# Attention, a max network and a gated network in one kernel: one operand block and two sums of the second pair are made during the product for y, and raw blocks, h's parts and g's stores are issued at other steps

## The chip, the cores and the metric

The kernel runs on one core of a Trainium2 chip. A core has five engines with a queue of instructions each: TensorE (PE: matmuls, with its weight loads PEld beside them), VectorE (DVE), ScalarE (ACT), GpSimd (POOL) and SyncE (SP), which here does nothing but issue DMAs. Each queue is worked off in order, and an instruction that waits holds all that stand behind it. The metric is the device time of one execution in microseconds (us): 1137.37 us, the median of 3 runs (1137.26 to 1139.59).

## The reference, cut to what matters

```python
def _attn_ref(q, k, v, cap):                    # 4 batches, 12 heads, 448 rows, head 64
    scores = cap * np.tanh(np.matmul(q, k.transpose(0, 1, 3, 2)) / np.sqrt(64) / cap)
    attn = np.exp(scores - np.max(scores, axis=-1, keepdims=True))
    return np.matmul(attn / (np.sum(attn, axis=-1, keepdims=True) + 1e-09), v)

x = attn_out.transpose(0, 2, 1, 3).reshape(1792, 768)
h = np.maximum(np.maximum(x @ w1, x @ w2), x @ w3)      # 768 x 768 each (float64 weights)
y = h @ w_out                                            # 1792 x 768
g = y @ w_gate                                           # 768 x 1536
out = (g * (1 / (1 + np.exp(-g))) * (y @ w_val)) @ moe2_w_out   # 1792 x 768
```

## The kernel before, in words

Each product is made of three fp32r matmuls: an operand is cut into a high part (ACT copies it to fp32r) and a low part (DVE or POOL subtracts the high part), and high x high, high x low and low x high are added up in PSUM. `parts_of` (L493 to L498) is the helper that cuts, so ACT's halves of all cuts have line L495 and those of DVE and POOL L498.

The weights are stored as float64. A raw block of 768 KB is fetched by SP (`fetch`, L455), and turned into fp32 in four steps, `one` to `four` (L469 to L486): ACT takes the absolute value of the high words (L470), DVE clamps and shifts (L475, L476), DVE puts the sign in and scales the low words (L479, L482), POOL adds both (L485). There are two buffers for raw blocks. So the fetch of block u+1 waits on SP until POOL's add of block u-1 has read its buffer.

The stages, in the order of time:

- 0 to 105 us: attention for batch 0, one pair of heads after the other, each in four slots. Per pair SP issues the loads of k, q and v (L82, L85, L74), the sums of the exponentials (`su`, L302), their inverses (`rd`, L313) and the inverses spread over the partitions (`rb`, L318). POOL multiplies by `rb` and cuts x (`finish`, L328 to L331). One conversion step of a raw block stands at the end of each slot.
- 105 to 420 us: attention for batch b+1, woven with x @ w1, w2, w3 of batch b. Block conversions and POOL's cuts of weights run beside it.
- 420 to 527 us: x @ w1, w2, w3 of batch 3. h was stored in DRAM by batch; it is fetched again (`hr`) and cut into `ha` (`split_h`, L646).
- 528 to 623 us: y = h @ w_out for batches 0 to 3, six products of 18 matmuls each. Batches 0 and 1 form pair 0, batches 2 and 3 pair 1.
- 623 to 948 us: the products for g and the value, in Strassen's form (Winograd's variant, 7 products in place of 8): per pair of batches seven operands B11, T2, T3, T1, B21, T4, B22 in `yo`, made of y's blocks `yf` by four sums (`sums_of_y`, L702), each cut in three slices; and per column block c = 0 to 11 seven weight operands (`ops_steps`). A product has 9 matmuls (`product`, L817). For c = 0 all seven products of pair 0 come first, then those of pair 1; from c = 1 on the pairs alternate.
- 948 to 1136 us: the last product, out = g @ w_out, of g read back from DRAM (`gr`) and cut.

The order of the work is written out by hand (tile pools set the waits for buffers). In the y stage, the cuts of h of batch b+1 stand one behind each product of batch b (L764 to L767). Pair 0's operands are made behind the last three products of batch 1 (L773 to L779): per slice a cut of B22, four sums and the cuts of T2, T3, T1 and T4, on POOL, ACT and DVE. Pair 1's are made by `y_steps` (L797 to L804) after the last product for y, behind the products of pair 0. Their buffer `yo1` lies where the pools of the y stage were.

Of the kernel before, what the change touches and what calls it, by code (L numbers as in the profile page):

```python
# [25 lines left out]
def attention_max_silu_kernel(ctx, tc, q, k, v, cap, w1, w2, w3, w_out, wg, wv, wo, out):  # L26
# [18 lines left out]
    nc = tc.nc  # L45
# [8 lines left out]
    capt = const.tile([P, 1], F32, name="capt")  # L54
    acap = const.tile([P, 1], F32, name="acap")
    ncap = const.tile([P, 1], F32, name="ncap")
    qsc = const.tile([P, 1], F32, name="qsc")
# [55 lines left out]
def program(ctx, tc, tensors, shared, general):  # L113
# [482 lines left out]
    with tc.manual_schedule():  # L596
# [49 lines left out]
        def split_h(b, kk):  # L646
# [4 lines left out]
            if kk + 4 < NF1:  # L651
                fetch_h(b, kk + 4)
# [49 lines left out]
        def sums_of_y(p, kk):  # L702

            b11, b12, b21, b22 = yf[p, 0, kk], yf[p, 1, kk], yf[p, 0, kk + 3], yf[p, 1, kk + 3]
            return dict(T1=b11, T3=b12, T2=b22, T4=b21), [
                lambda eng: less(eng, b11, b12, b11), lambda eng: less(eng, b12, b22, b12),
                lambda eng: less(eng, b22, b22, b11), lambda eng: less(eng, b21, b21, b22),
# [36 lines left out]

        events = {(0, 0): [split_next, convert_part], (0, 1): [convert_part]}
# [9 lines left out]
        for b in range(B):  # L755
            p, x = divmod(b, 2)
            for i in range(NK):
# [13 lines left out]
                if b == 0:  # L771
                    yo_part(0, "B11" if e < 3 else "B21", kk, y)
                if b == 1 and e >= 3:  # L773
# [4 lines left out]
                    for name, eng in zip(("T2", "T3", "T1", "T4"), (ve, po, ve, po)):  # L778
                        yo_part(0, name, kk, at[name], eng)  # L779
# [222 lines left out]
```

## Time and profile before

| what | value |
|---|---|
| median of 3 runs | 1137.37 us |
| the profiled execution: its time, its span | 1138.13 us, 1136.2 us |
| PE busy | 1090.2 us, 96% of the span |
| PE's weight loads busy | 941.3 us, 83% |
| DVE, POOL busy | 682.3 us, 682.7 us: 60% each |
| ACT busy | 510.1 us, 45% |

The execution is 1.9 us longer than the span, which runs from the first to the last instruction. A PE that is busy 96% of the time leaves 46 us in which it stood still; where these lie is read from the stretches of time below. A busy PE can still be slow: the granted clock (PEclk, 1.00 is 2.4 GHz) tells that.

### The profile page before, as it was taken

The page shows a single profiled execution, that of the slowest core. Times are in us where ns is not written, and L with a number is a line of the kernel's source. Part 1 is how long each engine was busy: PE and PEld are TensorE (multiplying, and loading weights), DVE is VectorE, ACT ScalarE, POOL GpSimd, SP SyncE. Part 2 cuts the span into 40 slices and gives each one's busy share as a digit, 9 for nine tenths or more (in the row PEclk, how much of TensorE's full clock was granted, in tenths as well). Part 3 has the DMA queues.
Part 4 walks back from the last instruction along what each step waited for, and adds up shares of the span by engine and source line. Part 5 has one row for each costly group of instructions (what it writes and reads, how often), then busy time and mean ns, then how long its engine had stood idle before and what let it go on. Part 6 is the DMA issues. An engine that isn't in the chain of part 4 may idle for free.

```text
span 1136.2 us, 15037 instructions
## 1 busy us (share of the span) xinstructions
PE 1090.2 (96%) x5480; PEld 941.3 (83%) x5480; DVE 682.3 (60%) x865; ACT 510.1 (45%) x789; POOL 682.7 (60%) x577
## 2 busy tenths in 40 slices
PE   7998998999999999999989789999999998999998
PEld 5444777888888889998979679999999998999997
DVE  2574999977776678764373956666676755211210
ACT  4876666677666762453353433323323224211210
POOL 1367999899878789985263566666655555211210
PEclk8999999999999999999989989999999999999999
DMA  4565444433434323443122022222232226333232
GB/s 113 134 170 134 118 122 125 131 101 105 135 106 118 116 82 117 161 129 105 33 78 66 0 89 88 88 99 103 92 112 98 88 82 192 97 110 100 84 93 64
DMA packets 167683, 118.67 MB, mean 104 GB/s; under 512 B 85680, under 2 KB 162992, under 8 KB 167600
## 3 DMA queue, kind: packets, MB, share of 16 engines
q1 hardware_dynamic: 167600, 117.62, 34.5%
q8 instruction: 45, 0.74, 0.3%
q14 instruction: 38, 0.31, 0.1%
HBM read 90.67 MB, written 26.82 MB: 103 GB/s over the span
## 4 chain that ended last, share of the span: by engine, by line
PE 76%; DVE 9%; POOL 4%; DMA 4%; ACT 3%; issue 2%; SPq 1%; DVEq 0%; POOLq 0%; ACTq 0%
PE ps_g L826 25%; PE ps_h L544 20%; PE ps_o L896 14%; PE ps_y L544 7%; PE pv L281 6%; PE sc L232 4%; POOL xp L328 1%; DVE el L256 1%; DVE yo L498 1%; DMA rb<-rd 1%; ACT e L246 1%; DMA raw<-in_moe_w_dram 1%; DVE xp L328 1%; DMA wo<-wod 1%; POOL yf L700 1%
## 5 line engine op out<-in xcount | busy, mean ns | idle before, releaser
L544 PE MATMUL ps_h<-x,ws 128*128 128x448 f32 x1296 | 294.3, 374 | 0.0
L544 PEld LDWEIGHTS ps_h<-x,ws 128*128 128x128 f32 x1296 | 241.1, 190 | 38.6 <-issue 18.1
L826 PE MATMUL ps_g<-yo,o_S 128*128 128x448 f32 x864 | 184.2, 369 | 4.5 <-DVE yo L498 1.9
L498 POOL TENSOR_TENSOR ws<-w,ws 128x384 fp32r<-128x384 f32 x144 | 181.7, 1269 | 10.6 <-ACT ws L495 1.6
L896 PE MATMUL ps_o<-wo,g 128*128 128x384 f32 x1008 | 177.3, 336 | 5.1 <-ACT g L495 2.7
L896 PEld LDWEIGHTS ps_o<-wo,g 128*128 128x128 f32 x1008 | 176.0, 189 | 6.5 <-ACT g L495 3.1
L826 PEld LDWEIGHTS ps_g<-yo,o_S 128*128 128x128 f32 x864 | 162.8, 189 | 21.7 <-DVE yo L498 2.6
L485 POOL TENSOR_TENSOR t<-t,raw 128x768 uint32<-128x768 uint32 x42 | 81.8, 1948 | 107.3 <-DVE raw L482 100.6
L826 PE MATMUL ps_g<-yo,o_A 128*128 128x448 f32 x648 | 140.0, 370 | 4.9 <-POOL yo L498 3.4
L826 PEld LDWEIGHTS ps_g<-yo,o_A 128*128 128x128 f32 x648 | 122.1, 189 | 18.2 <-POOL yo L498 4.2
L256 DVE TENSOR_TENSOR el<-e,eh 128x896 fp32r<-128x896 f32 x64 | 86.7, 1357 | 45.0 <-ACT eh L255 39.4
L498 POOL TENSOR_TENSOR g<-gr,g 128x384 fp32r<-128x384 f32 x28 | 32.5, 1181 | 113.0 <-ACT g L495 113.0
L246 ACT ACTIVATE e<-e,ncap,acap 128x896 f32<-128x896 f32 x96 | 99.4, 1036 | 0.6
L544 PE MATMUL ps_y<-ha,ws 128*128 128x448 f32 x432 | 90.8, 373 | 5.6 <-ACT ha L495 3.2
L238 ACT ACTIVATE e<-sc,qsc 128x896 f32<-128x896 f32 x96 | 86.7, 904 | 17.6 <-PE sc L232 17.4
L544 PEld LDWEIGHTS ps_y<-ha,ws 128*128 128x128 f32 x432 | 83.1, 193 | 13.3 <-ACT ha L495 3.5
L497 POOL TENSOR_SCALAR ws<-w 128x384 fp32r<-128x384 f32 x108 | 87.5, 810 | 0.2
L281 PE MATMUL pv<-eh,vs 128*128 128x448 f32 (+1 forms) x256 | 78.6, 389 | 2.5 <-ACT o L297 2.5
L498 DVE TENSOR_TENSOR g<-gr,g 128x384 fp32r<-128x384 f32 x28 | 23.9, 860 | 75.7 <-ACT g L495 75.5
L485 POOL TENSOR_TENSOR w<-w,raw 128x768 uint32<-128x768 uint32 x18 | 37.9, 2108 | 40.8 <-DVE raw L482 40.8
L470 ACT ACTIVATE t<-raw 128x768 f32<-128x768 f32 x42 | 37.6, 895 | 51.6 <-DMA raw<-in_moe_w_val_dram 42.7
L732 POOL TENSOR_TENSOR t<-t,t 128x384 f32<-128x384 f32 x36 | 39.9, 1109 | 31.2 <-DVE o_A L498 31.1
(113 smaller groups left out, 1560.9 us busy)
## 6 DMA issues: line engine op xcount, KB each, us to landing
raw<-in_moe_w_dram SPq DMA_DIRECT2D x18, 768.0 KB, 4.6
raw<-in_moe_w_out_dram SPq DMA_DIRECT2D x18, 768.0 KB, 5.0
gr<-gd SPq DMA_DIRECT2D x14, 768.0 KB, 4.9
raw<-in_moe_w_gate_dram SPq DMA_DIRECT2D x12, 768.0 KB, 4.3
raw<-in_moe_w_val_dram SPq DMA_DIRECT2D x12, 768.0 KB, 4.5
qn<-in_q_dram SPq DMA_DIRECT2D x48, 112.0 KB, 3.5
rb<-rd SPq DMA_DIRECT2D x48, 112.0 KB, 3.1
h<-ht SPq DMA_DIRECT2D x24, 224.0 KB, 2.0
```

Of the source, the lines that this page charges most:

```text
L232: nc.tensor.matmul(ps[:, j, :S], a[r, cols_], m[r], start=i == 0, stop=i == 2)
L238: nc.scalar.activation(ee[n][:, :w], ps[:, :w, :S], AF.Tanh, scale=qsc)
L246: nc.scalar.activation(t, t, AF.Exp, bias=ncap, scale=acap)
L256: nc.vector.tensor_sub(lo, t, f(hi))
L281: nc.tensor.matmul(pv[g][j][:, :S], a, m, start=c == 0 and x == 0, stop=c == 3 and x == len(ops) - 1,)
L485: nc.gpsimd.tensor_tensor(t, t, low, op=ALU.add)
L497: copier.tensor_scalar(hi, src, 1.0, 1.0, ALU.mult, ALU.mult)
L498: subtracter.tensor_tensor(lo, src, f(hi), op=ALU.subtract)
L544: nc.tensor.matmul(ps, a, m, start=kk == 0 and n == 0, stop=kk == NK - 1 and n == 2)
L732: nc.gpsimd.tensor_tensor(a[x], a[x0], a[x1], op=op)
L826: nc.tensor.matmul(ps, a[:, s0, k3], m[:, kk, s1], start=kk == 0 and j == 0, stop=kk == 2 and j == 2,)
L896: nc.tensor.matmul(po[s][x][:, :HW], a, m[:, x * HW : (x + 1) * HW], start=c == 0 and n == 0, stop=c == NF2 - 1 and n == 2,)
```

## The change

It has these parts:

1. B11 of pair 1 gets a buffer of its own (`b11_p`) that is there during the y stage. It is cut behind batch 2's first three products.
2. Pair 1's sums 0 (b12 - b11) and 1 (b12 - b22) are made by DVE behind batch 3's products (`early_sums`). After the y stage there remain: B22, sum 2, T2, T3, T1, B21 with sum 3, T4, all on ACT and DVE. Before, POOL had the subtractions for B22 and T4 and the sums 1 and 3.
3. h's blocks of batch b+1 are cut two at a time behind the first three products of batch b, and the first three are fetched one batch ahead. There are 3 fetch buffers in place of 4.
4. The fetch of the next raw block stands behind step `one` in place of step `clamp`, that is one step earlier.
5. The stores of g wait in a list and are issued up to two products later; around the last column block the fetch of g comes one step earlier and its cut one step later.
6. Four constants share one tile.

```diff
         def one():
             nc.scalar.activation(f(t), high.bitcast(F32), AF.Abs)
-
-        def clamp():
             if count[0] < min(count[1] + 2, len(real)):
                 fetch()
+
+        def clamp():
...
+        b11_p = pool(b11_pools, "b11", 1).tile([P, 3, 2, S], F32R, name="b11")
...
+        def early_sums(e, kk):
+
+            if e < 3:
+                made[kk] = sums_of_y(1, kk)
+                made[kk][1][0](nc.vector)
+            if (1, 1, kk) in yf and (1, 1, kk + 3) in yf:
+                made[kk][1][1](nc.vector)
...
-                if 1 <= b < B - 1:
-                    if i == 0:
-                        fetch_all(b + 1)
-                    split_h(b + 1, i)
+                if 1 <= b < B - 1 and i < 3:
+                    split_h(b + 1, 2 * i)
+                    split_h(b + 1, 2 * i + 1)
+                if b < B - 2 and i == 4:
+                    fetch_all(b + 2)
...
-                if b == 0:
-                    yo_part(0, "B11" if e < 3 else "B21", kk, y)
+                if x == 0 and (p == 0 or e < 3):
+                    yo_part(p, "B11" if e < 3 else "B21", kk, y)
+                if b == B - 1:
+                    early_sums(e, kk)
...
         y_steps = [
-            lambda: (y_part("B11"), y_sum(0, nc.vector)),
-            lambda: (y_part("B22", nc.gpsimd), y_sum(1, nc.gpsimd)),
-            lambda: y_sum(2, nc.vector),
-            lambda: y_part("T2"),
+            lambda: y_part("B22"), lambda: y_sum(2, nc.vector), lambda: y_part("T2"),
             lambda: y_part("T3"), lambda: y_part("T1"),
-            lambda: (y_part("B21"), y_sum(3, nc.gpsimd)), lambda: y_part("T4", nc.gpsimd),
+            lambda: (y_part("B21"), y_sum(3, nc.vector)), lambda: y_part("T4"),
         ]
...
+            while len(stores) > 1:
+                store()
...
-                nc.sync.dma_start(out=gd[:, c, 2 * p * S : (2 * p + 1) * S], in_=t[3])
+                stores.append((gd[:, c, 2 * p * S : (2 * p + 1) * S], t[3]))
...
-                at.setdefault(10, []).append(lambda: (fetch_g(rows[0]), fetch_g(rows[1])))
-                at.setdefault(12, []).append(lambda: [split_g(rows[0], y) for y in range(4)])
+                at.setdefault(8, []).append(lambda: [store() for _ in [*stores]])
+                at.setdefault(9, []).append(lambda: (fetch_g(rows[0]), fetch_g(rows[1])))
+                at.setdefault(13, []).append(lambda: [split_g(rows[0], y) for y in range(4)])
```

On DVE, at the end of batch 1's products for y, the kernel before has this (`yo0` are pair 0's operands, `ha2` the cut h of batch 2, `yf1_3` the y block 3 of batch 1):

```order
L498 TENSOR_TENSOR ha2_5512<-hr2_3_5510,ha2_5512 128x448
L498 TENSOR_TENSOR yo0_5319<-yf1_3_5588,yo0_5319 128x448
L700 TENSOR_TENSOR yf1_3_5588<-yf1_3_5588,yf0_0_5345 128x448
L498 TENSOR_TENSOR yo0_5319<-yf1_3_5588,yo0_5319 128x448
L498 TENSOR_TENSOR yo0_5319<-yf0_0_5345,yo0_5319 128x448
L498 TENSOR_TENSOR ha2_5512<-hr2_4_5515,ha2_5512 128x448
L498 TENSOR_TENSOR yo0_5319<-yf1_4_5625,yo0_5319 128x448
L700 TENSOR_TENSOR yf1_4_5625<-yf1_4_5625,yf0_1_5376 128x448
L498 TENSOR_TENSOR yo0_5319<-yf1_4_5625,yo0_5319 128x448
L498 TENSOR_TENSOR yo0_5319<-yf0_1_5376,yo0_5319 128x448
L498 TENSOR_TENSOR ha2_5512<-hr2_5_5540,ha2_5512 128x448
```

The changed kernel has there:

```order
L496 TENSOR_TENSOR ha2_5511<-hr2_3_5514,ha2_5511 128x448
L496 TENSOR_TENSOR ha2_5511<-hr2_4_5518,ha2_5511 128x448
L496 TENSOR_TENSOR ha2_5511<-hr2_5_5543,ha2_5511 128x448
L496 TENSOR_TENSOR yo0_5320<-yf1_3_5593,yo0_5320 128x448
L702 TENSOR_TENSOR yf1_3_5593<-yf1_3_5593,yf0_0_5346 128x448
L496 TENSOR_TENSOR yo0_5320<-yf1_3_5593,yo0_5320 128x448
L496 TENSOR_TENSOR yo0_5320<-yf0_0_5346,yo0_5320 128x448
```

The last two cuts of batch 2's h moved from behind pair 0's operands to the front of them.

On DVE, at the step from the y stage to the products for g, the kernel before has (`o0_S2` is a weight operand of c = 0, `yo1` are pair 1's operands, `yf2_0` and `yf3_0` y blocks of batches 2 and 3):

```order
L498 TENSOR_TENSOR o0_S2_5919<-t79_5792,o0_S2_5919 128x384
L498 TENSOR_TENSOR yo1_6012<-yf2_0_5710,yo1_6012 128x448
L498 TENSOR_TENSOR yo1_6012<-yf2_1_5737,yo1_6012 128x448
L498 TENSOR_TENSOR yo1_6012<-yf2_2_5764,yo1_6012 128x448
L700 TENSOR_TENSOR yf2_0_5710<-yf3_0_5972,yf2_0_5710 128x448
L700 TENSOR_TENSOR yf2_1_5737<-yf3_1_5999,yf2_1_5737 128x448
L700 TENSOR_TENSOR yf2_2_5764<-yf3_2_5866,yf2_2_5764 128x448
L700 TENSOR_TENSOR yf3_3_5889<-yf3_3_5889,yf2_0_5710 128x448
L700 TENSOR_TENSOR yf3_4_5914<-yf3_4_5914,yf2_1_5737 128x448
L700 TENSOR_TENSOR yf3_5_5943<-yf3_5_5943,yf2_2_5764 128x448
L837 TENSOR_TENSOR qn1_64<-ps_g0_0_1_6048,qn0_63 128x448
```

The changed kernel has there:

```order
L702 TENSOR_TENSOR yf2_1_5746<-yf3_1_6010,yf2_1_5746 128x448
L702 TENSOR_TENSOR yf3_1_6010<-yf3_4_5922,yf3_1_6010 128x448
L496 TENSOR_TENSOR o0_S2_5927<-t79_5803,o0_S2_5927 128x384
L496 TENSOR_TENSOR yo1_6025<-yf3_3_5899,yo1_6025 128x448
L496 TENSOR_TENSOR yo1_6025<-yf3_4_5922,yo1_6025 128x448
L496 TENSOR_TENSOR yo1_6025<-yf3_5_5951,yo1_6025 128x448
L702 TENSOR_TENSOR yf3_3_5899<-yf3_3_5899,yf2_0_5713 128x448
L702 TENSOR_TENSOR yf3_4_5922<-yf3_4_5922,yf2_1_5746 128x448
L702 TENSOR_TENSOR yf3_5_5951<-yf3_5_5951,yf2_2_5775 128x448
L864 TENSOR_TENSOR qn1_61<-ps_g0_0_1_6051,qn0_60 128x448
```

Two sums of the last y block now stand ahead of the weight operand S2; B11's cuts are gone from here and B22's, which POOL made, stand in their place, with three sums in place of six.

On SP, in the attention of batch 0, the kernel before has (`vp0` is v of a pair of heads, `raw3` a raw block of weights):

```order
L85 DMA vp0_179<-in_v_dram 64x64
L302 DMA su2_580<-o2_554 112x1x4 x2
L318 DMA rb1_583<-rd1_186 64x448 x2
L455 DMA raw3_588<-in_moe_w1_dram 128x6x128
L82 DMA kn0_65<-in_k_dram 128x3x64
```

The changed kernel has there:

```order
L83 DMA vp0_176<-in_v_dram 64x64
L453 DMA raw3_567<-in_moe_w1_dram 128x6x128
L300 DMA su2_579<-o2_551 112x1x4 x2
L316 DMA rb1_582<-rd1_183 64x448 x2
L80 DMA kn0_62<-in_k_dram 128x3x64
```

The raw block, which waits for POOL's add of the block before last, moved ahead of the sums and of the spread inverses.

## Rows read from the trace of the kernel before

**Rows 1.** The profile's page: its first line

```profile
span 1136.2 us, 15037 instructions
```

**Rows 2.** Stretches: length; PE, PEld, DVE, ACT, POOL busy (instructions); PEclk, DMA share, GB/s

```profile
0.00:100.00 100.00, 89.07 (x397) 48.53 (x398) 49.01 (x78) 69.83 (x82) 39.30 (x45) 0.95 0.55 139
100.00:210.00 110.00, 100.35 (x492) 79.08 (x493) 97.33 (x98) 71.68 (x92) 103.46 (x84) 0.94 0.44 123
...
575.00:585.00 10.00, 5.15 (x14) 4.36 (x15) 7.67 (x7) 5.00 (x11) 8.48 (x7) 0.70 0.08 23
...
635.00:670.00 35.00, 25.60 (x104) 20.34 (x103) 22.91 (x37) 14.73 (x29) 19.09 (x17) 0.90 0.05 20
...
945.00:980.00 35.00, 29.89 (x156) 28.32 (x155) 12.56 (x13) 13.06 (x22) 18.16 (x12) 0.95 0.59 181
```

**Rows 3.** Timeline, PE, y stage: start, us, instruction, count, [idle before <- releaser]

```profile
527.89 47.10 PE L544 MATMUL ps_y<-ha,ws 128*128 128x448 f32 x231 [0.72 <-DVE ht L570]
...
578.15 0.47 PE L544 MATMUL ps_y<-ha,ws 128*128 128x448 f32 x1 [3.17 <-ACT ha L495]
580.32 2.24 PE L544 MATMUL ps_y<-ha,ws 128*128 128x448 f32 x5 [1.70 <-DVE ha L498]
```

**Rows 4.** Timeline, PE, first products for g

```profile
623.44 2.00 PE L826 MATMUL ps_g<-yo,o_A 128*128 128x448 f32 x9
...
655.48 3.35 PE L826 MATMUL ps_g<-yo,o_A 128*128 128x448 f32 x8 [3.40 <-POOL yo L498]
...
667.38 2.93 PE L826 MATMUL ps_g<-yo,o_S 128*128 128x448 f32 x13 [0.50 <-DVE o_S L498]
```

**Rows 5.** The chain that ended last: start, us, what

```profile
138.69 5.52 DMA raw<-in_moe_w_dram
...
181.76 4.46 DMA raw<-in_moe_w_dram
...
667.38 273.70 PE ps_g L826 x1330
```

**Rows 6.** Timeline, DVE, around the y stage's end

```profile
567.11 0.63 DVE L700 TENSOR_TENSOR yf<-yf,yf 128x448 f32<-128x448 f32 x1
...
624.69 0.56 DVE L498 TENSOR_TENSOR o_S<-t,o_S 128x384 fp32r<-128x384 f32 x1 [2.68 <-ACT o_S L495]
...
628.60 8.10 DVE L700 TENSOR_TENSOR yf<-yf,yf 128x448 f32<-128x448 f32 x6
...
637.16 1.68 DVE L498 TENSOR_TENSOR yo<-yf,yo 128x448 fp32r<-128x448 f32 x3
```

**Rows 7.** Timeline, POOL, the same place

```profile
643.46 1.83 POOL L485 TENSOR_TENSOR t<-t,raw 128x768 uint32<-128x768 uint32 x1 [7.78 <-DVE raw L482]
...
653.21 1.13 POOL L851 TENSOR_TENSOR kn<-kn,qn 128x448 f32<-128x448 f32 x1
654.30 3.31 POOL L498 TENSOR_TENSOR yo<-yf,yo 128x448 fp32r<-128x448 f32 x3
```

**Rows 8.** Timeline, SP and POOL, one pair of heads in batch 0

```profile
50.92 1.85 POOL L485 TENSOR_TENSOR w<-w,raw 128x768 uint32<-128x768 uint32 x1
...
52.02 1.93 SPq L302 DMA_DIRECT2D su<-o  x2
...
54.05 1.19 SPq L318 DMA_DIRECT2D rb<-rd  x2
...
55.33 0.54 SPq L455 DMA_DIRECT2D raw<-in_moe_w_dram  x1
...
56.92 2.95 POOL L328 TENSOR_TENSOR xp<-o,rb 64x448 f32<-64x448 f32 x2 [4.15 <-DMA rb<-rd]
...
61.88 1.86 POOL L485 TENSOR_TENSOR w<-w,raw 128x768 uint32<-128x768 uint32 x1
```

**Rows 9.** Timeline, the step to the last product: PE

```profile
951.16 5.57 PE L896 MATMUL ps_o<-wo,g 128*128 128x384 f32 x22 [2.73 <-ACT g L495]
957.54 17.26 PE L896 MATMUL ps_o<-wo,g 128*128 128x384 f32 x98 [0.82 <-DVE g L498]
```

More of the change, by code (lines that the diff above doesn't have):

```diff
@@ L53, in attention_max_silu_kernel @@
     ident = const.tile([P, P], F32, name="ident")
[L54 to L57, printed above, removed]
+    four = const.tile([P, 4], F32, name="four")
+    capt, acap, ncap, qsc = (four[:, i : i + 1] for i in range(4))
     qn = [const.tile([P, 4, 2, D], F32, name=f"qn{i}") for i in range(2)]
@@ L657, in fetch_all @@
         def fetch_all(b):
-            for kk in range(4):
+            for kk in range(3):
                 fetch_h(b, kk)
@@ L702, in sums_of_y, with b2 @@
         def sums_of_y(p, kk):
[L704 to L707, printed above, removed]
+            b11, b12 = yf[p, 0, kk], yf[p, 1, kk]
+            def b2(x):
+                return yf[p, x, kk + 3]
+            return dict(T1=b11, T3=b12, T2=lambda: b2(1), T4=lambda: b2(0)), [
+                lambda eng: less(eng, b11, b12, b11), lambda eng: less(eng, b12, b2(1), b12),
+                lambda eng: less(eng, b2(1), b2(1), b11), lambda eng: less(eng, b2(0), b2(0), b2(1)),
             ]
@@ L743, in ops_steps @@
             ]
+        def early_sums(e, kk):
[4 more added lines that the diff above has]
+                made[kk][1][1](nc.vector)
+        made = {}
         events = {(0, 0): [split_next, convert_part], (0, 1): [convert_part]}
@@ L783, in program @@
         yo1_pools = ctx.enter_context(ExitStack())
-        yo[1] = pool(yo1_pools, "yo1", 1).tile([P, 7, 3, 2, S], F32R, name="yo1")
+        yo1 = pool(yo1_pools, "yo1", 1).tile([P, 6, 3, 2, S], F32R, name="yo1")
+        yo.update({(1, x): yo1[:, n] for n, x in enumerate(with_[1:])})
         K3 = range(3)
-        made = {kk: sums_of_y(1, kk) for kk in K3}
         def y_part(name, eng=nc.vector):
-            src = dict(B11=(0, 0), B21=(0, 3), B22=(1, 3)).get(name)
             for kk in K3:
-                yo_part(1, name, kk, yf[1, src[0], src[1] + kk] if src else made[kk][0][name], eng)
+                if name[0] == "B":
+                    src = yf[1, int(name[2]) - 1, kk + 3]
+                else:
+                    src = made[kk][0][name]
+                    src = src() if name in ("T2", "T4") else src
+                yo_part(1, name, kk, src, eng)
         def y_sum(n, eng):
@@ L807, in program, with store @@
         ct = [None]
-        tmp, Z = {}, {}
+        tmp, Z, stores = {}, {}, []
+        def store():
+            dst, src = stores.pop(0)
+            nc.sync.dma_start(out=dst, in_=src)
         def spare(c, p, k):
@@ L929, in program @@
                 both.sort(key=lambda x: x[1])
-                for step in y_steps[:2]:
-                    step()
-                for i, step in enumerate(y_steps[2:]):
+                y_steps.pop(0)()
+                for i, step in enumerate(y_steps):
                     at.setdefault(i, []).insert(0, step)
@@ L947, in program @@
                     step()
+        while stores:
+            store()
         for y in range(4):
```

21 lines of the change are left out of this document (13 added, 8 removed).

## The prediction

> **What bounds the kernel now.** I read the page first [rows 1], then the stretches of time with the clock granted in each [rows 2], then PE's timeline where a stretch is short of work, and last the engine that PE waited for. The reader is to see in the stretches that 40 of PE's 46 idle us lie in the five shown, which are four places; PE is the bound in the rest, and only these four can give anything.
>
> - The attention of batch 0 and the first stretch of batch 1 (0 to 210 us): PE stands still for 10.9 and 9.7 us [rows 2], DVE or POOL or SP being late.
> - The y stage, at the start of batch 2's products: PE waits 3.17 us for ACT's and 1.70 us for DVE's cut of the last block of h [rows 3], and the clock falls to a mean of 0.70 in these 10 us [rows 2], that is to the lower level for most of what follows. The whole loss: 231 matmuls took 47.10 us, 0.204 each [rows 3]; the stage has 24 products of 18 = 432, which at that pace is 88.1 us; from 527.89 to the first matmul for g at 623.44 [rows 4] it took 95.55. So 7.4 us are lost.
> - The first products for g: 16 products of 9 matmuls and two more, 146, lie between 623.44 and 667.38 [rows 4], 43.94 us. At the pace of what follows, 273.70 us for 1330 or 0.206 each [rows 5], they would take 30.0. So 13.9 us are lost: 9.4 as idle time, the rest at a clock of 0.90 on the mean [rows 2]. The longest wait, 3.40 us, is for T4, whose low half POOL makes in 3.31 us after three sums [rows 4, 7].
> - The step to the last product: 5.1 us idle [rows 2], of which 2.73 us wait for g to come back from DRAM and 0.82 for a cut of it [rows 9].
>
> **The y stage, batch 2 (part 3 of the change).** The blocks of h that came late were the fifth and sixth, which stood on ACT and DVE behind pair 0's operands. Now all six stand ahead of these, and the first fetches start one batch earlier. A cut costs about 0.6 us on each engine (as the 0.56 of a half in [rows 6]); six behind three products of 18 x 0.204 = 3.7 us fit. The buffer of `ha2` is free when batch 0's products end. So the wait goes, and the clock has no cause to fall: -7.4 us. What is late next is pair 0's operands: they hold the copies of y behind them on ACT, but with eight PSUM banks PE can run eight products, 29 us, ahead. Then batch 3's h: its six cuts start after them, and the last fetch now stands behind a raw block. I cost this at nothing: PE asks for the sixth block only 324 + 15 matmuls after the stage's start, at 597 us, a whole batch (22 us) after the cuts of pair 0's operands began to hold ACT. It is up to 5 us, a raw block's landing [rows 5], if that cover is gone.
>
> **The step from y to g (parts 1 and 2).** POOL's share falls away (3.31 us for T4, as much for B22, and the sums), and DVE gets all halves. Its list from the end of y until T4 is ready: 8 sums (two in the y stage's last step, three of sum 2, three of sum 3), 19 low halves (S2, then three each of B22, T2, T3, T1, B21, T4), six additions of pair 0's products and four conversion steps. A sum by itself took 0.63 us, a half 0.56 [rows 6]; an addition I take as a sum, the four conversion steps as 2.6 us together (their bounds are four halves, 2.2, and 4 x 1.35). This is 8 x 0.63 + 19 x 0.56 + 6 x 0.63 + 2.6 = 22.1 us, and 0.8 until the last y block is copied (S2's half now starts 1.25 us after the first matmul for g, behind ACT's half of it [rows 4, 6]): 22.9. PE wants T4 after 12 products, 12 x 9 x 0.206 = 22.2 us, and its last slice 1.2 us later. So DVE is ready about when PE asks; the other operands are earlier in both lists. I take 2 us of stall for it, because each conversion or multiplication on POOL can hold a DVE instruction. S2 of c = 0 now waits for two sums on DVE: 0.8 + 2 x 0.63 + 0.56 = 2.6 us, where PE wants its low half after 11 matmuls, 2.3 us: 0.5. The wait for S2 of c = 1 (0.89 before the 0.50 of [rows 4]; 1.4 in all) stays. Rest 3.9 us, gain 13.9 - 3.9 = 10.0. The bounds: a rest of 0.5 us, and one of 10 (5 us of POOL's holding, 1.8 for S2 at slow sums, 3 for c = 1).
>
> The rows show what a hold costs: six sums took 8.10 us, 1.35 each, while POOL made its own [rows 6, 7], against 0.63 alone. The Trainium skill, SBUF, "Who interferes with whom", has it as a rule that speaks against this change: a VectorE instruction with two SBUF inputs and a GpSimd instruction that reads SBUF take one read interface in turn, and the one that is later is held for the whole instruction. By that rule every POOL instruction that is left (1.83, 1.13 twice, and about two for c = 1's operands) is added to DVE's 22.9, some 5 us; by the row, where 4.53 us of POOL beside six sums added 8.10 - 6 x 0.63 = 4.3, it is the same size. I keep 2 in the sum since most of these fall where DVE waits or after T4, and 5 as a rival.
>
> **The raw blocks (part 4).** In the attention of batch 0 the fetch now stands ahead of `su` and `rb` on SP. It waits for POOL's add of the block before last, and that add stands on POOL behind `finish`, which waits for `rb`. This closes a ring: add ends; raw issue 0.6; two `su` 1.3; `rb` issued, and landed 2.9 us later (54.05 to 56.92); from there to the end of the next add 6.8 (56.92 to 63.74) [rows 8]. That is 11.7 us with the hand-over, where a pair now takes 10.96 (from add to add in [rows 8]). `rb` starts about 0.8 us late at first and some 0.8 more in each of three rounds; the round with four more loads (21 issues of 0.6 us each) takes 0.7 of it back: +2.7 us. Its bounds: 0, if the pairs have slack that these rows don't show, and 5, if SP must wait in the later rounds too.
>
> From 105 us on, DVE is 97.3 us busy of 110 [rows 2], so at most 12.7 can be gained. Twice a raw block's landing, 5.52 and 4.46 us, stands on the chain [rows 5], both after SP had issued other things first: four loads of v before the first (four issues, 2.4 us), and before the second a store of h that waited for DVE. Both fetches now stand ahead of these. I take 2.3 + 1.4 = 3.7 off, at most 10.0, at least nothing: the fetches that wait for POOL's add hold q, `rd` and v behind them. Together the attention changes by +2.7 - 3.7 = -1.0, from +5 to -10.
>
> **The stores and the tail (parts 5 and 6).** In between, PE was never idle for them, so nothing, as long as PE's 275 us hide them; a store that came a product late and held a buffer would cost one product, 1.9 us. At the end the fetch of g stays behind the same three loads of the output weights, so 2.73 us stay; the cut of g no longer holds ACT's and DVE's work for the last product, so the 0.82 goes and perhaps more: -1.0, from -2.5 to +1 (a store of g now stands behind a load that waits). The constants: nothing.
>
> **Sum.** -7.4 - 10.0 - 1.0 - 1.0 = -19.4, on the execution's own 1138.1 us (1136.2 of span and 1.9 around it): 1118.7. The runs' median lies 0.8 lower, so 1118.0; I say 1118.5.
>
> **Rivals.**
>
> - DVE stays the bound at the step to g, POOL's rest holding it: rest 10 instead of 3.9, 1124.6. For it: 1.35 us per sum [rows 6]. Against: the POOL instructions that made it so are the ones removed. Chance 0.14.
> - The ring in the attention costs its 5 us and the second stretch gives nothing: +5 instead of -1, 1124.5. For it: POOL's 103 us of 110 [rows 2]. Chance 0.16.
> - The wait for h only moves to batch 3, whose last block lands behind a raw block: 5 us back, 1123.5. Chance 0.06. With it counts that the change doesn't do what it says, y's operands not being what is late.
> - Slower: SP. Eleven raw fetches in the first 210 us stand earlier and wait for POOL with loads, sums or `rd` behind them. If each keeps PE waiting for h us, the attention costs 11h against the 18.4 gained elsewhere. It turns at h = 1.7, and at 2.4, POOL's add and the issue of the block [rows 8] in full, the time is 1137.4 - 18.4 + 26.4 = 1145.4. Against: in the ring above a fetch costs 0.8, and q lands a whole pair ahead. Chance 0.04.
>
> **How the numbers follow.** The forecast has 0.60: 1118.5, by itself from 1113 to 1123. To 1128 lie two of the first three rivals at once; below, the bounds of y to g (3.4) and of the attention (9) reach to 1109 when half of the latter comes. Range 1110 to 1128. A measurement of this kernel tells about 0.2%, 2.3 us, from no change: faster needs less than 1135.1, which all cases but the last give, with some 0.02 for several at once: faster 0.93, the same 0.03, slower 0.04.
>
> **What would show it.** In the changed kernel's profile: no PE wait for `ha` at the first products of batch 2, and a clock of 1.00 there; the first 146 matmuls for g in some 34 us; no subtraction of `yo` or `yf` for pair 1 on POOL, and DVE's sums near 0.63; SP waiting at the raw fetch for POOL's add in batch 0's attention, `rb` up to 3 us later there; the raw landings after 105 us gone from the chain. I am wrong if the stall at T4 stays above 6 us, if the wait for `ha` comes back at batch 3, or if PE's idle time before 210 us grows by more than 5.

## The result, and the profile after

The changed kernel takes 1123.57 us (median of 4 runs, 1122.27 to 1124.79), the kernel before 1138.48 (4 runs, 1137.26 to 1140.44): a ratio of 0.9867, 95% interval 0.9844 to 0.9890. It is faster, by 14.9 us; forecast were 1118.5 us and a range of 1110 to 1128.

The sum held better than its terms. By stages of the profiled executions, in us (the third column is the first experiment below, the changed kernel with the raw fetches put back):

| stage | before | changed | fetch put back | forecast of the change |
|---|---|---|---|---|
| start to first matmul for y | 527.89 | 531.36 | 527.23 | -1.0 |
| 432 matmuls for y | 95.55 | 88.02 | 87.65 | -7.4 |
| first 146 matmuls for g | 43.94 | 37.48 | 35.35 | -10.0 |
| other 1366 matmuls for g | 281.05 | 277.41 | 280.20 | 0 |
| end of these to the last matmul | 182.43 | 180.99 | 180.4 | -1.0 |

The changes are +3.47, -7.53, -6.46, -3.64 and -1.44, together -15.6, the difference of the spans (1136.2 and 1120.6). The y stage came as forecast; attention got longer, the step to g gained less, and the products for g got faster although nothing was forecast to touch them.

The boundary at 146 matmuls, which the prediction chose, hides something. The last two of the 146 are the first two for the weight operand S2 of c = 1, which PE waited for, and behind that wait the clock can fall. The next 52 matmuls took 10.79, 12.07 and 12.86 us in the three kernels. So over the first 198 matmuls for g the three took 54.72, 49.55 and 48.21 us, and from there to the start of the last one 269.90, 264.97 and 266.98.

The page's first line and the stretches answer to [rows 1, 2]; the last stretch lies 15 us earlier than there.

```profile
span 1120.6 us, 15038 instructions
```

```profile
0.00:100.00 100.00, 84.18 (x378) 45.24 (x378) 48.74 (x76) 64.07 (x75) 34.33 (x40) 0.97 0.53 135
100.00:210.00 110.00, 100.83 (x484) 77.88 (x485) 96.52 (x95) 74.41 (x95) 103.47 (x84) 0.92 0.44 122
575.00:585.00 10.00, 10.00 (x51) 9.26 (x51) 5.59 (x5) 2.99 (x6) 9.11 (x8) 1.00 0.00 0
635.00:670.00 35.00, 30.67 (x142) 27.26 (x142) 26.27 (x45) 12.13 (x23) 17.13 (x13) 0.95 0.22 69
930.00:965.00 35.00, 32.00 (x165) 30.88 (x164) 14.03 (x14) 12.94 (x22) 18.37 (x12) 0.90 0.68 206
```

PE's idle time in the first 100 us grew from 10.9 to 15.8 us, the next 110 gave 0.5 back. At 575 us the hole of 4.85 us is gone and the clock is 1.00. PE's timeline, which answers to [rows 3, 4, 9], has no wait for `ha` any more; what is left before and after the products for g is this:

```profile
531.36 8.98 PE L542 MATMUL ps_y<-ha,ws 128*128 128x448 f32 x43 [0.72 <-DVE ht L568]
...
619.38 1.96 PE L851 MATMUL ps_g<-yo,o_A 128*128 128x448 f32 x9
622.77 0.67 PE L851 MATMUL ps_g<-yo,o_S 128*128 128x448 f32 x2 [1.43 <-ACT o_S L493]
624.51 5.27 PE L851 MATMUL ps_g<-yo,o_S 128*128 128x448 f32 x25 [1.06 <-DVE o_S L496]
...
644.79 1.89 PE L851 MATMUL ps_g<-yo,o_A 128*128 128x448 f32 x8 [0.29 <-DVE yo L496]
...
655.68 0.67 PE L851 MATMUL ps_g<-yo,o_S 128*128 128x448 f32 x2 [3.53 <-ACT o_S L493]
656.86 5.37 PE L851 MATMUL ps_g<-yo,o_S 128*128 128x448 f32 x18 [0.51 <-DVE o_S L496]
...
936.74 1.65 PE L923 MATMUL ps_o<-wo,g 128*128 128x384 f32 x4 [2.47 <-ACT g L493]
938.92 1.33 PE L923 MATMUL ps_o<-wo,g 128*128 128x384 f32 x3 [0.53 <-DVE g L496]
```

The 3.40 us for T4 shrank to 0.29. Both waits for the weight operand S2 (c = 0 at 622 us, c = 1 at 655) grew: 2.5 and 4.0 us.

One round of the ring in batch 0, on SP and POOL, answers to [rows 8]:

```profile
51.51 1.85 POOL L483 TENSOR_TENSOR w<-w,raw 128x768 uint32<-128x768 uint32 x1
...
53.39 0.37 SPq L453 DMA_DIRECT2D raw<-in_moe_w_dram  x1
53.85 1.22 SPq L300 DMA_DIRECT2D su<-o  x2
55.12 1.23 SPq L316 DMA_DIRECT2D rb<-rd  x2
...
58.56 3.13 POOL L326 TENSOR_TENSOR xp<-o,rb 64x448 f32<-64x448 f32 x2 [5.20 <-DMA rb<-rd]
...
63.51 1.85 POOL L483 TENSOR_TENSOR w<-w,raw 128x768 uint32<-128x768 uint32 x1
...
65.39 0.37 SPq L453 DMA_DIRECT2D raw<-in_moe_w_dram  x1
```

POOL's add ends at 53.36 and the raw block leaves SP at 53.39: it had waited for that. The next round starts 12.00 us later (53.39 to 65.39).

### The profile page after: what moved, and what is told of

It reads as the page before. It is cut to its first block, busy times and chain, and to the rows that moved or that the text cites. A ratio compares the mean times of both kernels' runs of the same rounds, so it can differ in the third digit from the quotient of the medians.

```text
span 1120.6 us, 15038 instructions
## 1 busy us (share of the span) xinstructions
PE 1078.3 (96%) x5480; PEld 939.5 (84%) x5480; DVE 694.1 (62%) x877; ACT 511.1 (46%) x789; POOL 674.5 (60%) x565
## 4 chain that ended last, share of the span: by engine, by line
PE 78%; DVE 7%; POOL 5%; ACT 3%; issue 3%; DMA 3%; SPq 1%; DVEq 0%; POOLq 0%
PE ps_g L851 25%; PE ps_h L542 21%; PE ps_o L923 16%; PE pv L279 6%; PE sc L230 4%; PE ps_y L542 3%; POOL xp L326 2%; DMA rb<-rd 2%; DVE el L254 1%; ACT e L244 1%; POOL yf L702 1%; PE pk L208 1%; DVE raw L480 1%; DVE yo L496 1%; POOL yo L496 1%
## 5 line engine op out<-in xcount | busy, mean ns | idle before, releaser
L542 PE MATMUL ps_h<-x,ws 128*128 128x448 f32 x1296 | 290.8, 371 | 0.6 <-ACT ht L565 0.6
L851 PE MATMUL ps_g<-yo,o_S 128*128 128x448 f32 x864 | 181.1, 367 | 6.5 <-ACT o_S L493 5.0
L254 DVE TENSOR_TENSOR el<-e,eh 128x896 fp32r<-128x896 f32 x64 | 89.6, 1405 | 39.1 <-ACT eh L253 33.5
L851 PE MATMUL ps_g<-yo,o_A 128*128 128x448 f32 x540 | 113.4, 364 | 0.3 <-DVE yo L496 0.3
L851 PEld LDWEIGHTS ps_g<-yo,o_A 128*128 128x128 f32 x540 | 101.2, 188 | 8.3 <-DVE yo L496 0.7
L244 ACT ACTIVATE e<-e,four 128x896 f32<-128x896 f32 x96 | 99.4, 1035 | 0.6
L236 ACT ACTIVATE e<-sc,four 128x896 f32<-128x896 f32 x96 | 86.7, 904 | 18.0 <-PE sc L230 17.9
L495 POOL TENSOR_SCALAR ws<-w 128x384 fp32r<-128x384 f32 x108 | 92.4, 856 | 0.2
L253 ACT ACTIVATE eh<-e 128x896 fp32r<-128x896 f32 x64 | 55.1, 860 | 3.1 <-ACT e L244 1.1
L875 ACT ACTIVATE ct<-ct 128x448 f32<-128x448 f32 x23 | 13.3, 579 | 94.3 <-DVE ct L874 94.3
```

The lines of the kernel that those rows point to most:

```text
L236: nc.scalar.activation(ee[n][:, :w], ps[:, :w, :S], AF.Tanh, scale=qsc)
L244: nc.scalar.activation(t, t, AF.Exp, bias=ncap, scale=acap)
L253: nc.scalar.activation(hi, t, AF.Copy)
L254: nc.vector.tensor_sub(lo, t, f(hi))
L495: copier.tensor_scalar(hi, src, 1.0, 1.0, ALU.mult, ALU.mult)
L542: nc.tensor.matmul(ps, a, m, start=kk == 0 and n == 0, stop=kk == NK - 1 and n == 2)
```

## The experiments

All ran beside the kernel before, which had medians of 1137.12 to 1137.82 us. Ratios are to it, with 95% intervals.

| kernel | median, range (us) | ratio |
|---|---|---|
| 1 changed, raw fetch back at `clamp` | 1117.86, 1115.91 to 1118.67 | 0.9820, 0.9806 to 0.9834 |
| 2 changed, early fetch in batch 0 only | 1122.80, 1120.27 to 1125.21 | 0.9872, 0.9851 to 0.9892 |
| 3 changed, early fetch later only | 1121.94, 1119.60 to 1124.70 | 0.9870, 0.9852 to 0.9888 |
| 4 before, h's parts only | 1130.63, 1128.97 to 1133.38 | 0.9941, 0.9926 to 0.9957 |
| 5 before, y's operands only | 1126.70, 1125.85 to 1130.09 | 0.9908, 0.9891 to 0.9926 |
| 6 before, stores only | 1137.73, 1135.51 to 1139.34 | 1.0000, 0.9989 to 1.0011 |
| 7 before, constants only | 1132.87, 1129.44 to 1134.08 | 0.9952, 0.9936 to 0.9968 |
| 8 as 1, 32 bytes ahead of the weight operands | 1124.38, 1122.63 to 1125.84 | 0.9885, 0.9867 to 0.9903 |
| 9 as 1, 32 bytes at the other end | 1125.63, 1122.09 to 1125.73 | 0.9889, 0.9873 to 0.9905 |
| 10 as 1, S2 made earlier | 1114.89, 1113.34 to 1116.91 | 0.9807, 0.9792 to 0.9823 |
| 11 as 1, stores and fetch of g first | 1117.38, 1116.25 to 1122.12 | 0.9836, 0.9815 to 0.9857 |
| 12 as 10, fetch and cut of g first | 1111.25, 1109.69 to 1111.49 | 0.9762, 0.9740 to 0.9784 |

### The early raw fetch: 1, 2 and 3

```diff
# 1
         def one():
             nc.scalar.activation(f(t), high.bitcast(F32), AF.Abs)
-            if count[0] < min(count[1] + 2, len(real)):
-                fetch()
         def clamp():
+            if count[0] < min(count[1] + 2, len(real)):
+                fetch()
# 2: as 1, and in one()
+            if count[1] < 7 and count[0] < min(count[1] + 2, len(real)):
+                fetch()
# 3: as 2, with count[1] >= 13
```

Expected of 1: 

> The changed kernel with the fetch of the next raw block put back from step one to step clamp, nothing else. Theory (the ring add, fetch, su, rb, finish, add costs the first 105 us): rb is issued every 10.7 us again instead of 12.0, the hand-over from batch 0's attention goes from 215.7 back to about 209.7 us, and the first matmul for y from 531.4 to 527.9; the time is 1123.6 - 3.5 = 1120.1 us. Rival (the later hand-over comes from something else in the change, such as the shifted buffers, or from the chip): rb every 12.0 us, 1123.6 us.

Expected of 2: 

> The changed kernel with the early fetch (step one) for the seven blocks that batch 0's attention converts alone, and the fetch at step clamp from then on. Theory (the ring of batch 0 is the whole loss of the early fetch): rb every 12.0 us, first matmul for y at 531.4, the time that of the changed kernel, 1123.6 us; the fetch put back everywhere gave 1117.9. Rival (the later early fetches cost as much, which the 1121.9 us of the kernel with them alone suggest): part of the loss goes, 1119 to 1121 us. Second rival (the loss of the ring is made up by slack in the woven stretch): 1118 us.

Expected of 3: 

> The changed kernel with the fetch at step clamp for the thirteen blocks of batch 0's attention and at step one from the fourteenth block on. Theory (the early fetch is harmful in the ring alone and worth something after it: 2.6 of the 6.05 us lost by the hand-over had come back by the y stage): hand-over at 209.7, first matmul for y at 531.4 - 6.05 = 525.3 us, time 1117.5 us. Rival (what came back is only the slack of the woven stretch, the early fetch gives nothing there): the same as with the fetch put back everywhere, first matmul for y at 527.9, 1120.1 us.

Measured: putting the fetch back takes 5.7 us off the changed kernel. SP in kernel 1 issues `rb` ahead of the raw block again, and 11.1 us apart in place of 12:

```profile
53.55 1.19 SPq L316 DMA_DIRECT2D rb<-rd  x2
54.83 0.54 SPq L453 DMA_DIRECT2D raw<-in_moe_w_dram  x1
...
64.69 1.19 SPq L316 DMA_DIRECT2D rb<-rd  x2
```

The first matmul for y comes at 527.23 as expected. But kernel 1 gains 2.1 us more in the first 146 matmuls for g (35.35 against 37.48 us; 1.3 over the first 198), which neither theory had. Kernel 2, with the ring alone, is 4.9 us slower than 1, its first matmul for y at 533.5 us. Kernel 3 is 4.1 us slower than 1, though its profiled run, the fastest of its four, has the y stage start at 526.9, no later than kernel 1. (The bound of 13 blocks in kernel 3 takes in batch 0's seven and six of batch 1; the text on record calls all thirteen batch 0's.) So the early fetch costs in both places, and the two (9.0 us) don't add up to the 5.7 of both together. For the later cost the profiles show one place: with the early fetch (changed, kernel 3) PE waits 1.43 and 0.89 us for ACT's and 1.06 twice for DVE's cut of S2, with the late fetch (1, 2, 5) only for DVE's, 1.35 to 1.63. S2's makers stand on POOL behind the add of the last raw block, which ends 3.1 us ahead of the first matmul for g in the changed kernel and 5.8 us ahead in kernel 1. That the raw blocks hold up S2's makers there is read from these profiles; no run tests it by itself. Kernel 3 takes 1.5 us more than kernel 1 over the first 198 matmuls for g; where the rest of its loss lies isn't settled.

### The parts by themselves: 4, 5 and 6

```diff
# 4: part 3 of the change alone, as in its diff
# 5: parts 1 and 2 alone; for space also
-            hr[b, kk] = seq.tile([P, S], F32, tag="hr", name=f"hr{b}_{kk}", bufs=4)
+            hr[b, kk] = seq.tile([P, S], F32, tag="hr", name=f"hr{b}_{kk}", bufs=3)
+    four = const.tile([P, 4], F32, name="four")
# 6: part 5 alone, as in its diff
```

Expected of 4: 

> The kernel before with the change of h's parts alone: two cuts at a time behind the first three products, three fetch buffers, the first fetches one batch ahead. Theory (the wait for h in batch 2 is the whole loss of the y stage): the stage from 95.55 to 88.0 us, nothing given back in the first 146 matmuls for g (43.9 us), time 1138.5 - 7.5 = 1131.0 us. Rival (the operands of pair 1 don't come earlier, so the earlier start of g is paid back as a longer stall there): the stage 88.0, the first 146 matmuls up to 51.5 us, time 1138.5 us.

Expected of 5: 

> The kernel before with parts 1 and 2 alone (B11 of the second pair and two sums during the y stage, POOL's subtractions given to DVE), and what they need for space: three fetch buffers for h in place of four and the constants in one tile. Theory (they gain 6.5 us at the step from y to g, not the 10.0 predicted, and the constants' tile its 4.7 us by the pace of the matmuls): 1137.6 - 4.7 - 6.5 = 1126.4 us, the first 146 matmuls for g in 37.5 us. Rival (the cuts of h, still one behind each product, stand behind B11's cuts and come later, so that the wait for h in the y stage grows): y stage above 95.6 us, 1129 us or more.

Expected of 6: 

> The kernel before with part 5 alone (the stores of g issued up to two products later, the fetch of g a step earlier, its cut a step later). Theory: nothing between 667 and 945 us, the pace of the products for g still 0.206 us each, about 1.0 us off the step to the last product: 1136.6 us. Rival (the later stores are what made the products for g faster): 0.203 each, 3.6 us less, 1133.0 us.

Measured: in 4 the y stage takes 87.6 us (528.9 to 616.5) and the first 146 matmuls 43.95 as before: nothing is given back, and the gain is 7.0 us. In 5 these 146 take 35.24 us, 8.7 less than before and better than its theory, which had taken the changed kernel's 37.5. Its y stage is 96.6 us, 1.1 longer, but not as its rival has it: the waits for h are those of the kernel before, 3.17 and 1.70 us [rows 3]. What is slower is the pace behind them: the last 200 matmuls take 44.35 us where the kernel before has 43.28, and the median matmul of the stage is 368 ns where it has 365. PE's timeline of kernel 5:

```profile
576.72 0.48 PE L542 MATMUL ps_y<-ha,ws 128*128 128x448 f32 x1 [3.17 <-ACT ha L493]
578.89 44.35 PE L542 MATMUL ps_y<-ha,ws 128*128 128x448 f32 x200 [1.69 <-DVE ha L496]
```

In 6 nothing moves that can be measured: at most 1.3 us to either side, and its products for g have the old pace.

### The constants: 7, 8 and 9

```diff
# 7: part 6 of the change alone, as in its diff
# 8: as 1, and
-    four = const.tile([P, 4], F32, name="four")
+    four = const.tile([P, 12], F32, name="four")
# 9: as 1, and
+    pad = pool(ctx, "pad", 1, side="right").tile([P, 8], F32, name="pad")
     res = pool(res_pools, "res", 1, side="right")
```

Expected of 7: 

> The kernel before with the four constants in one tile alone, which moves every buffer behind them by a few bytes. Theory (the place of the buffers sets the pace of the products for g): the 1366 matmuls from 667 us on at 0.2031 us each as in the changed kernel, 3.6 us less, time 1134.9 us. Rival (the pace comes from another part, the buffers of the second pair's operands or the later stores, or from the run): 0.2057 each, time 1138.5 us.

Expected of 8: 

> The changed kernel with the fetch back at step clamp, and the tile of the constants 48 bytes long in place of 16, so that every buffer behind it, the weight operands among them, starts 32 bytes later: at a multiple of 64 bytes as in the kernel before, where they stood 32 bytes beside one in the changed kernel. Theory (the weight operands' place within 64 bytes sets the pace): median matmul of the products for h 366 ns and for g 368 ns as before, in place of 363, time 1117.9 + 4.7 = 1122.6 us. Rival (the pace comes from something else that the shorter tile moves, or only from a distance of 96 bytes): 363 ns, 1117.9 us.

Expected of 9: 

> The changed kernel with the fetch back at step clamp, and 32 bytes put beside the buffers that are laid out from the other end of SBUF: x, the first pair's operands and y's blocks then start at a multiple of 64 bytes, the weight operands stay 32 bytes beside one. Theory (only the weight operand's place within 64 bytes sets the pace): median matmul of the products for h 363 ns as without the pad, time 1117.9 us. Rival (what counts is that both operands of a matmul stand at the same place within 64 bytes, which the y stage's equal pace in all kernels suggests): the products for h 366 ns or more and pair 0's products for g 366, 1121 us.

Measured: the tile of constants alone is worth 4.8 us. Its other 1366 matmuls for g take 277.5 us, nearly as in the changed kernel. The view is the list of one tile's forms: durations of PE's matmuls in ns, least, median and most, and the first and last start. First kernel 6, which has the old layout, then 7, 8 and 9:

```profile
L544 PE MATMUL ps_h<-x,ws x1296: 358/366/741, 107.1 to 528.0; 128*128 128x448 f32 x186
```

```profile
L542 PE MATMUL ps_h<-x,ws x1296: 360/363/740, 105.9 to 526.1; 128*128 128x448 f32 x186
```

```profile
L542 PE MATMUL ps_h<-x,ws x1296: 360/369/739, 107.2 to 530.5; 128*128 128x448 f32 x186
```

```profile
L543 PE MATMUL ps_h<-x,ws x1296: 360/369/742, 108.0 to 531.5; 128*128 128x448 f32 x186
```

In the layout of the built program (it is fixed when the kernel is built; no trace shows it) each of the four small tiles took 32 bytes of a partition, so everything behind them now starts 96 bytes earlier. The weight operands start at byte 22272 before, a multiple of 64, and at 22176 after, 32 beyond one. The moving operands x and `yo0` are laid out from the other end and start 32 beyond a multiple of 64 in both. In kernel 8 the weights are back on a multiple of 64 (22208) and the median is 369; in kernel 9 the weights stay and x moves onto a multiple of 64 (127424), and it is 369 too. So the place of the weights alone isn't it, as the theory for 8 and 9 had it; the rival for 9 is right: a matmul is faster when both operands stand at the same place within 64 bytes than when they stand 32 apart, the two distances that these kernels have. All nine kernels where x and the weights do so (the changed one, 1 to 3, 5, 7, 10 to 12) have 363 ns, and all five where they don't have 366 (before, 4, 6) or 369 (8, 9).

The products for g say the same pair by pair. In kernel 8's last column block, the 126 matmuls at the end of g, pair 1's operands stand as the weights do and pair 0's don't. (In this block the pairs don't alternate: pair 1's seven products come first, then pair 0's.) Pair 0 first, then pair 1:

```profile
L851 PE MATMUL ps_g<-yo,o_S x34: 369/369/369, 923.5 to 934.0; 128*128 128x448 f32 x34
...
L851 PE MATMUL ps_g<-yo,o_S x34: 362/365/369, 910.7 to 921.0; 128*128 128x448 f32 x34
```

The time of the products for g falls into four levels. From the 199th matmul on, where the clock is full in all kernels, to the start of the last one they take 269.90 us with the old layout (before, 4, 6), 264.97 to 264.98 with the new one (changed, 2, 5, 7, 10, 11, 12), 268.02 in 8 and 9, and 266.98 in 1 and 3, which have the new layout too. So the layout is worth 4.9 us here; the last section has the exception.

### Two waits that were left: 10, 11 and 12

```diff
# 10: as 1, and in ops_steps
-                lambda: (tile_of("S1"), tile_of("A12"), cut("S1", po)),
-                lambda: (tile_of("A22"), cut("A22", ve)),
-                lambda: (make("S2", "A22", "A22", "S3"), cut("A12", ve)),
-                lambda: (cut("S2", ve), make("S4", "A12", "A12", "S2")),
+                lambda: (make("S2", "S3", "A22", "S3"), tile_of("S1"), tile_of("A12"), cut("S1", po)),
+                lambda: cut("S2", ve),
+                lambda: (tile_of("A22"), cut("A22", ve)),
+                lambda: (cut("A12", ve), make("S4", "A12", "A12", "S2")),
# 11: as 1, and around the last column block
-                at.setdefault(8, []).append(lambda: [store() for _ in [*stores]])
-                at.setdefault(9, []).append(lambda: (fetch_g(rows[0]), fetch_g(rows[1])))
-                at.setdefault(13, []).append(lambda: [split_g(rows[0], y) for y in range(4)])
+                at.setdefault(7, []).insert(0, lambda: [store() for _ in [*stores]])
+                at.setdefault(7, []).insert(1, lambda: (fetch_g(rows[0]), fetch_g(rows[1])))
+                at.setdefault(12, []).append(lambda: [split_g(rows[0], y) for y in range(4)])
# 12: 10 and 11, with
+                at.setdefault(11, []).insert(0, lambda: [split_g(rows[0], y) for y in range(4)])
```

Expected of 10: 

> The changed kernel with the fetch back at step clamp, and the second weight operand (S2) made as soon as S3 is cut, in the place of S3's source, in place of behind the cut of A22. Theory (the two waits for S2 that are left at the step from y to g, some 1.4 and 3.4 us, come from S2 standing behind A22's cut, which itself waits for DVE's early sums or for a free buffer): both waits go, the first 146 matmuls for g take some 33 us in place of 37, time 1117.9 - 4 = 1114 us. Rival (DVE's whole list is the bound there, as one rival of the prediction had it): the waits move to T4, the stretch stays at 37 us, 1117.9 us.

Expected of 11: 

> The changed kernel with the fetch back at step clamp, and at the last column block the last two stores of g and the fetch of g issued ahead of the fetches of output weights that stand in front of them, and the cut of g one product earlier. Theory (the wait for g at the step to the last product, 2.7 us, is the store's and the fetch's queue on SP behind the load of output weights, which waits for a buffer): g lands some 3.5 us earlier, the waits of 2.7 and 0.9 us go, time 1117.9 - 3 = 1115 us. Rival (the landing of the fetch of g, some 8 us beside other loads, is set by the DMA engines, or the wait moves to the output weights): 1117.9 us, with a wait for wo in place of the one for g.

Expected of 12: 

> The changed kernel with the fetch back at step clamp, S2 made earlier, the last two stores and the fetch of g ahead of the output weights on SP, and the cut of g two products earlier than in the changed kernel, ahead of the fourth cut of output weights. Theory (with the cut of g behind the landing of the fourth output weight on ACT, the earlier fetch of g alone only turned its wait into one for DVE's cuts): the waits for g fall from 3.7 us to under 1, time 1114.9 - 2.5 = 1112.4 us. Rival (the DMA engines are full there, and the output weights of the next steps come late instead): waits for wo of 2 to 3 us, 1115 us.

Measured: kernel 10 gains 3.0 us over 1. The first 146 matmuls take 33.78 us, 1.6 less; the wait for S2 of c = 0 is gone, that of c = 1 fell from 3.0 to 0.8, and 1.1 us appeared at T4, so the rival has its share. PE's timeline of kernel 10:

```profile
616.74 5.56 PE L851 MATMUL ps_g<-yo,o_S 128*128 128x448 f32 x27
...
639.70 1.89 PE L851 MATMUL ps_g<-yo,o_A 128*128 128x448 f32 x8 [1.06 <-DVE yo L496]
...
647.89 11.59 PE L851 MATMUL ps_g<-yo,o_S 128*128 128x448 f32 x54 [0.83 <-ACT o_S L493]
```

The same 54 matmuls in kernel 1, and 5 us behind S2's wait in kernel 1 and in kernel 10:

```profile
649.05 14.20 PE L851 MATMUL ps_g<-yo,o_S 128*128 128x448 f32 x54 [3.02 <-ACT o_S L493]
```

```profile
650.00:655.00 5.00, 4.93 (x14) 4.25 (x14) 1.70 (x4) 2.77 (x5) 4.22 (x4) 0.50 0.56 168
```

```profile
650.00:655.00 5.00, 5.00 (x26) 4.65 (x26) 2.09 (x4) 2.38 (x6) 3.52 (x4) 1.00 0.21 58
```

So the shorter wait for S2 also kept the clock at its upper level, where PE does 26 matmuls in 5 us in place of 14. This is 2.3 us in the 52 matmuls behind the 146, more than the 1.6 us within them; neither the theory nor its rival had it.

Kernel 11 alone isn't told from 1. ACT's timeline there shows why: the cut of g stood behind the cut of an output weight that waited for its landing. The fetch of g left SP at 918.8 in place of 925.2 us, and the cut began only at 928.58.

```profile
927.83 0.84 ACT L493 ACTIVATE wo<-wo 128x768 fp32r<-128x768 f32 x1 [1.70 <-DMA wo<-wod]
928.58 1.75 ACT L493 ACTIVATE g<-gr 128x384 fp32r<-128x384 f32 x4
```

With that cut moved ahead too, kernel 12 is the fastest of all, 3.6 us under 10 and 26 under the kernel before. Both theories were partly right: ACT's wait for g is gone, and PE waits for output weights instead, as the rival had it. PE's waits in kernel 12 from 910 us on, in us (sum, times, longest):

```profile
PE ps_o L923 <- POOL wo L496: 1.9, 2, 1.3
PE ps_o L923 <- DVE g L496: 1.1, 1, 1.1
PE ps_o L923 <- ACT wo L493: 0.4, 1, 0.4
```

That is 3.4 us idle, hardly less than the 3.7 of kernels 1 and 10. Part of the gain is in the clock, as the stretches of kernel 12, of kernel 1 and of kernel 10 show (the third number from the end is the granted clock):

```profile
920.00:930.00 10.00, 8.86 (x48) 8.15 (x47) 6.74 (x10) 6.76 (x13) 6.55 (x5) 1.00 0.72 222
930.00:940.00 10.00, 9.38 (x53) 9.06 (x54) 2.86 (x3) 2.77 (x4) 7.38 (x5) 1.00 0.58 192
940.00:950.00 10.00, 8.65 (x49) 8.02 (x47) 2.17 (x3) 3.15 (x5) 3.40 (x2) 1.00 0.76 209
```

```profile
930.00:940.00 10.00, 6.32 (x27) 5.62 (x26) 8.15 (x7) 7.04 (x13) 9.07 (x8) 0.83 0.80 234
```

```profile
930.00:940.00 10.00, 10.00 (x50) 10.00 (x49) 6.61 (x5) 5.07 (x8) 7.06 (x6) 0.83 0.60 192
```

In kernel 1 PE waited 2.73 and 0.94 us within 5 us and the clock fell to a mean of 0.83, partly the lower level. Kernel 10 has the same (2.67 and 1.00 us). In kernel 12 four waits of at most 1.3 us lie over 22 us and it stayed at 1.00. A mean of 0.83 over 10 us is 1.7 us of work lost, about half of the 3.6; where the other half lies isn't shown.

## Why the prediction was right in its sum and wrong in three steps

- **The y stage, batch 2: right.** Forecast -7.4, measured -7.53 in the changed kernel and 7.0 us with that part alone. Nothing moved to batch 3.
- **The step from y to g: the gain was forecast too large.** Forecast were 10.0 us. The first 146 matmuls gained 6.5 in the changed kernel and 8.6 and 8.7 with the late fetch (kernels 1 and 5); with the 52 behind them, where the clock fell, the gains are 5.2, 6.5 and 6.5. The failed step is the rest of 3.9 us. T4 cost 0.29 in place of 2, S2 of c = 0 2.5 in place of 0.5, S2 of c = 1 4.0 in place of 1.4, and the low clock behind S2 of c = 1 another 1.3 to 2.2 that were put at nothing. I had taken S2 as bound by two sums on DVE. But POOL makes it, and POOL waited 1.69 us for DVE's cut of A22, which stands ahead of S2. Kernel 10 makes S2 ahead of that cut, and its first 198 matmuls gain 10.3 us on the kernel before, the size of the forecast. The early fetch has a share, too: the changed kernel is 2.1 us behind kernel 1 here (1.3 over 198 matmuls), a cost at a place where I had not looked for it. POOL's timeline of the changed kernel (the two are the makers of S2 and S4):

```profile
620.92 2.58 POOL L738 TENSOR_TENSOR t<-t,t 128x384 f32<-128x384 f32 x2 [1.69 <-DVE o_A L496]
```

- **POOL's hold on DVE: there, but misread.** It was seen once: DVE's last early sums took 1.38 us each beside POOL's makers of S2 and S4, and 0.56 in three sums alone.

```profile
621.23 2.75 DVE L702 TENSOR_TENSOR yf<-yf,yf 128x448 f32<-128x448 f32 x2
...
641.98 1.69 DVE L702 TENSOR_TENSOR yf<-yf,yf 128x448 f32<-128x448 f32 x3
```

  In the kernel before, the prediction set 4.53 us of POOL against the 4.3 us by which six sums were slower (628.60 to 636.70 us). Two rows of POOL lie beside these sums, not one, so it was 7.1 us (628.60 to 635.69). By these rows the sums lost less than POOL's whole time beside them.

```profile
627.02 4.17 POOL L498 TENSOR_TENSOR yo<-yf,yo 128x448 fp32r<-128x448 f32 x3 [0.85 <-ACT yo L495]
631.16 4.53 POOL L700 TENSOR_TENSOR yf<-yf,yf 128x448 f32<-128x448 f32 x3
```

- **Attention: the sign was wrong, by two steps.** A round of the ring is as worked out, 12.0 us where 11.7 were forecast. The first failed step is how often it runs: the +2.7 counted three rounds and took 0.7 back in the one with four more loads (its own terms, 0.8 + 3 x 0.8 - 0.7, give 2.5). But that round took 13.73 us, where it had taken 13.65, and gave nothing back; `rb` of the sixth pair came 5.9 us late where up to 3 was said. PE's idle time in the first 100 us grew by 4.9, near the bound of 5 that the prediction gave for SP waiting in the later rounds too. SP's timeline, the kernel before and the changed one:

```profile
99.23 1.15 SPq L318 DMA_DIRECT2D rb<-rd  x2
```

```profile
105.10 1.23 SPq L316 DMA_DIRECT2D rb<-rd  x2
```

  The second failed step is that the later early fetches would take 3.7 us off raw landings. The landings did leave the chain, but the second stretch of [rows 2] stayed at 9 us idle: other work was as late. Kernel 3, which has the later early fetches alone, starts the y stage only 0.3 us earlier than kernel 1. Against the same kernel with the fetch put back the first matmul for y is 4.1 us later in the changed one, and the whole change of the fetch costs 5.7 us, not a gain of 1.0. My second rival said this of the mechanism. Its time, 1124.5, is near the measured 1123.6 only because the constants paid.
- **The constants: "nothing" was wrong.** They are 4.8 us by themselves, in the profiled run 0.7 before the y stage and 3.5 in the last 1366 products for g. I had asked what the tile's instructions cost and not what moves behind it. The Trainium skill, "TensorE: Matmul & The Clock Gate", "Step-by-step: what each phase is for", holds that the weight load and the moving operand have independent read ports, so that loading the next weights takes nothing from the running matmul. By that alone one would not expect the place of one against the other to matter; here it is worth 3 to 6 ns of 363, and the measurement decides.
- **Stores and tail: not shown.** Forecast -1.0; part 5 alone is 1.000 of before, within 1.3 us, so its sign stays open. The wait for g stayed at 2.47 us, as said.

That the sum came within 5 us and into the range is in part luck: the 4.8 us of the constants, which were put at nothing, nearly offset the 5.7 us of the fetch. None of the prediction's three signs of being wrong came (T4 at 0.29 us, no wait for `ha`, PE's idle time before 210 us up by 4.4 where 5 was the limit), so they were too coarse to find these errors.

By the parts: h 7.0, y's operands with the constants 11.1, less 5.7 for the fetch, make 12.4 of the 14.9 us. The remaining 2.5 are in no single part; the four intervals, 1.6 to 2.6 us to either side each, are wide enough to hold them.

## What to carry to other kernels

A prefetch that is issued one step earlier on a queue worked off in order takes its wait with it: ask what stands behind it there, and whether that is what the wait itself depends on. An edit that frees or adds a few bytes of SBUF moves every buffer behind it; compare the median duration of one matmul form before explaining a gain by the edit. And when an operand is late, look at what its maker stands behind on the engine before making the maker faster.

## What the runs showed that was not expected

- The pace of a matmul depends on where its two operands stand to each other within 64 bytes: 363 ns at the same place, 366 or 369 ns at 32 bytes' difference, in fourteen kernels, each profiled once. Kernels 8 and 9 differ from 1 by 32 bytes alone and are 6.5 and 7.8 us slower. Why it is 366 in one case and 369 in the other is open.
- Place isn't all. Where both operands are laid out from the same end and stand alike, the pace was mostly 365 ns, but pair 1's products for g took 368 in the profiled runs of kernels 1 and 3 (2.0 us in all), and the y stage 368 in kernel 5 and 369 in kernel 12, with buffers at the same bytes as in kernels that had 365. In the kernel before, pair 1 had 368 as well. The cause isn't settled.
- Several short waits spread over 22 us left the granted clock at 1.00, where nearly the same sum within 5 us took it to a mean of 0.83. What decides is not settled by these runs: behind the waits for S2 of c = 1 the clock stayed at 1.00 in the kernel before (0.89 and 0.50 us) and fell to 0.69 in kernel 7 (1.02 and 0.51 us, 667 to 672 us).
